# Key loads issued by ScalarE, scaled queries written in tile order by GpSimd, the factor of u by VectorE's reciprocal

## The chip, the cores and the metric

The kernel runs on one core of one Trainium2 chip. The time is that of one execution on the device, in microseconds (us). Three runs of the kernel before took 1848.44, 1849.12 and 1851.25 us, so the median is 1849.12 us. The profiled execution, from which all rows below come, took 1851.55 us. The program's instructions span 1849.8 us of it.

## What is computed

Attention over pooled keys, followed by a feed-forward layer with a SoLU activation and a layer norm. All inputs and outputs are float32 or wider (`moe_w_in` and `moe_w_out` arrive as float64).

```
kv_pool = kv.reshape(B, H//4, 4, W//4, 4, C).mean(axis=(2, 4))      # 4 batches, 768 keys of 128
k = v   = kv_pool.reshape(B, -1, C) @ w_sr
s = (q @ k.T) / sqrt(128);  a = softmax(s)                          # 12288 queries per batch
x = a @ v
h = x @ w_in;  solu = h * softmax(h)                                # 1024 columns
out = ((solu - mean) / sqrt(var + 1e-6) * g_ln) @ w_out
```

## The kernel before, in words

The 4 x 12288 queries are cut into 384 tiles of 128. Four tiles make a group (96 groups), and 96 tiles make a batch. The products are made from float16 pairs: a number is kept as a high half and a low half, and three products replace one. The first batch's scores use float32r pairs instead of float16 pairs (`wide(g)`).

One loop runs over 384 slots. In slot n several tiles are in work at different stages:

- the scores of tile n+1 (TensorE, L580), their maximum (VectorE, L601), the exponential and the high half (ScalarE, L602, L604), the low half (VectorE, L612), and a transpose of both halves by DMA, `pT<-phl` (L615);
- the product with the values for a group (TensorE, L640), written out as `xh` by ScalarE (L647) and `xl` by VectorE (L652);
- the hidden layer of tile n-9 (TensorE, L693), its maximum (VectorE, L701), its exponential `e` (ScalarE, L717), `u` = h times e times a factor per row (VectorE, L731), the halves of u (GpSimd, L748 and L755), and their transpose by DMA, `uT<-uhl` (L770);
- the last product of tile n-13 (TensorE, L821), which reads uT, and once per group the scaling and the store (L844, L853).

The order of every engine's instructions is the order in which the code records them (`manual_schedule`); nothing is rearranged, and each engine takes its instructions in that order. A DMA is also issued in the order of the engine that issues it. Before the change every DMA but one small load at the start is issued by SyncE (SP), so all share one queue: per slot one `pT` and one `uT` transpose, per group one load of queries (L528) and one store of results (L853).

While one batch is in work, the keys of the next are prepared. `kv_plan` places 16 loads of 384 KB each over the slots (`kv_load`, L225). GpSimd adds each load to a running sum in two halves (`kv_add`, L240). Six loads of the second batch (`SOON`) are issued before the loop; the other 42 stand in the loop, at the end of a slot whose number is a multiple of four, from slot 8 to slot 252. The last batch (tiles 288 to 383) has no next one, so no such loads or sums.

Three small steps belong to the change. `q_scale` (L540) multiplies a group's queries by a factor in place, contiguously, on GpSimd; `q_split` (L548, ScalarE) rounds them to float16 and `q_low` (L561, GpSimd) makes the low half. Both of the latter read the queries in steps of 128 elements (`by_tile`), so that one row of each tile stands beside those of the other three. In the first batch `q_scale` does nothing. `values_norm` (L661, GpSimd) makes two products of the softmax's sum per group, `values_recip` (L672, VectorE) inverts them, and `values_recip_u` (L678, ScalarE) multiplies one of the two by a factor `bb[:, 0:1]` to get the factor of u.

Of the kernel before, what the change touches and what calls it, by code (L numbers as in the profile page):

```python
# [67 lines left out]
def kernel(  # L68
# [38 lines left out]
    def float64_parts(raw, name):  # L107


        pair = raw.rearrange("p (f two) -> p f two", two=2)  # L110
        lo, hi = pair[:, :, 0], pair[:, :, 1]
        top = wrk.tile([P, DFF], F32, tag="u", name=f"top_{name}", bufs=5)
        if name == "in":
            rest = wrk.tile([P, DFF], F32, tag="u", name="rest_in", bufs=5)
        else:
            rest = bat.tile([P, 2 * NK], F32, tag="acc", name="rest_out", bufs=1)[:, :DFF]
        ex = wrk.tile([P, DFF], I32, tag="e", name=f"ex_{name}")
        sgn = wrk.tile([P, DFF], I32, tag="e", name=f"sgn_{name}")
        scalar = nc.vector.tensor_scalar
        both = nc.vector.tensor_tensor  # L120
        and_, shr = ALU.bitwise_and, ALU.logical_shift_right
        return top, rest, [
            partial(scalar, ex, hi, 20, 0x7FF, op0=shr, op1=and_),
            partial(scalar, ex, ex, -896.0, 0.0, op0=ALU.add, op1=ALU.max),
            partial(scalar, ex, ex, 255.0, 2.0**23, op0=ALU.min, op1=ALU.mult),
            partial(
                nc.vector.scalar_tensor_tensor,
                ex,
                hi,
                -0x80000000,  # L130
                ex,
                op0=and_,
                op1=ALU.bitwise_or,
            ),
            partial(scalar, sgn, hi, 0xFFFFF, 3, op0=and_, op1=ALU.logical_shift_left),
            partial(both, top.bitcast(I32), ex, sgn, op=ALU.bitwise_or),
            partial(
                nc.vector.scalar_tensor_tensor,
                rest,
                lo.bitcast(U32),  # L140
                2.0**-52,
                ex.bitcast(F32),
                op0=ALU.mult,
                op1=ALU.mult,
            ),
        ]
# [4 lines left out]
    def kv_alloc(b):  # L151
        for n, w, dt, bufs in (
# [3 lines left out]
            ("vf", NK, F32, 1),  # L156
        ):
            state[n, b] = bat.tile([P, w], dt, tag=n, name=f"{n}_{b}", bufs=bufs)
        for n, w in (("knm", 3), ("sv", 2), ("bb", 5), ("kq", 3), ("dg", P)):
            state[n, b] = (  # L160
                state[n, 0]
                if 0 < b < B
                else bat.tile([P, w], F32, tag=n, name=f"{n}_{b}", bufs=1)
            )
# [57 lines left out]
    def kv_first_t(half):  # L222
        nc.scalar.copy(half_of("kT", 0, half), state["pk0", half][:, :384])

    def kv_load(b, pos):  # L225

        t = dmt.tile([P, 2, 384], F32, tag="kvc", name=f"kv_{b}_{pos}", bufs=9)
        r, two = divmod(pos, 2)
        nc.sync.dma_start(
            t, kv[b - 1, r, :, two * NK : (two + 1) * NK].rearrange("p (h k) -> p h k", h=2)  # L230
        )
        state["kv", b, pos] = t
# [122 lines left out]
    def kv_bound0(part):  # L355
# [10 lines left out]
        else:  # L366
# [2 lines left out]
            small(bb[:, 2:3], bb[:, 1:2], 1e-9)  # L369
            small(bb[:, 3:4], knm[:, 2:3], 2.0**5, wsc)  # L370
            small(bb[:, 4:5], bb[:, 3:4], -1.0)
            small(sv[:, 1:2], sv[:, 1:2], knm[:, 2:3], 2.0**5 / (SC * SC))

    def kv_scale_v(b, part):
# [12 lines left out]
    def kv_bound(b, part):  # L387
# [20 lines left out]
        else:  # L408
            nc.vector.tensor_scalar(knm[:, 2:3], knm[:, 2:3], 2.0**5, None, op0=ALU.mult)
            nc.vector.tensor_scalar(bb[:, 3:4], knm[:, 2:3], wsc, None, op0=ALU.mult)  # L410
            nc.vector.tensor_scalar(bb[:, 4:5], bb[:, 3:4], -1.0, None, op0=ALU.mult)
            nc.vector.tensor_scalar(sv[:, 1:2], sv[:, 1:2], knm[:, 2:3], None, op0=ALU.mult)

    def kv_diag(b, half):
# [125 lines left out]
    def q_scale(g):  # L540
        if wide(g) or NG <= g:
            return
        qf = state["qf", g // QL][:, (g % QL) * 512 : (g % QL + 1) * 512]
        nc.gpsimd.tensor_scalar(
            qf, qf, state["kq", g // GPB][:, 1:2], 1.0, op0=ALU.mult, op1=ALU.mult
        )

    def q_split(g):  # L548
        if NG <= g < NG + GPB:
# [5 lines left out]
        else:  # L555
            qh = grp.tile([P, 512], F16, tag="qh", name=f"qh_{g}")
            ql = grp.tile([P, 512], F16, tag="ql", name=f"ql_{g}")
        nc.scalar.copy(in_tiles(qh), by_tile(qf))
        state["q", g] = (qh, ql)

    def q_low(g):  # L561
# [2 lines left out]
        qf = state["qf", g // QL][:, (g % QL) * 512 : (g % QL + 1) * 512]  # L564
        qh, ql = state["q", g]
        high = qh.bitcast(F32) if wide(g) else qh
        nc.gpsimd.tensor_tensor(in_tiles(ql), by_tile(qf), in_tiles(high), op=ALU.subtract)  # L567


    def scores_pe(t):  # L570
# [89 lines left out]

    def values_norm(g):  # L661
        b = g * GT // TPB
        zz = grp.tile([P, 2, GT], F32, tag="zz", name=f"zz_{g}", bufs=2)
        rz = grp.tile([P, 3, GT], F32, tag="rz", name=f"rz_{g}", bufs=3)
        z, bb = state.pop(("z", g)), state["bb", b]
        for k in range(2):
            nc.gpsimd.tensor_scalar(
                zz[:, k, :], z, 1e-9, bb[:, 3 + k : 4 + k], op0=ALU.add, op1=ALU.mult
            )
# [2 lines left out]
    def values_recip(g):  # L672

        zz, rz = state.pop(("zz", g))
        nc.vector.reciprocal(rz[:, 0:2, :], zz)  # L675
        state["rz", g] = [rz[:, k, :] for k in range(3)]

    def values_recip_u(g):  # L678
        rz = state["rz", g]
        nc.scalar.activation(rz[2], rz[0], AF.Copy, scale=state["bb", g * GT // TPB][:, 0:1])  # L680
        state["z2", g] = grp.tile([P, GT], F32, tag="z2", name=f"z2_{g}", bufs=3)
        state["v3", g] = grp.tile([P, GT], F32, tag="v3", name=f"v3_{g}", bufs=3)

# [208 lines left out]
        kv_first_load(*divmod(n, 8))  # L892
    q_load(1)
    for pos in SOON:
        kv_load(1, pos)
    nc.scalar.mul(w_sr16, wsr, 1.0 / RR)

    warm = ps_o.tile([P, 512], F32, tag="o", name="warm")
# [422 lines left out]
```

## Time and profile before

| what | us |
|---|---|
| median of three runs | 1849.12 |
| the profiled execution | 1851.55 |
| its span | 1849.8 |
| TensorE matmuls busy (PE) | 1821.7 |
| ScalarE busy (ACT) | 1783.7 |
| VectorE busy (DVE) | 1769.8 |
| GpSimd busy (POOL) | 1683.1 |

Busy time is a sum over the whole span. Four engines are busy for more than nine tenths of it, so the shares alone do not say which one is waited for. For that the trace is read by stretches and by waits. The source lines of the rows are those of the kernel before.

### The profile page before, as it was taken

Reading aid. Unit: us, or ns where it says so; the run is one execution under the profiler, and the core shown is the slowest. Engines: PE = TensorE matmul, PEld = TensorE weight load, DVE = VectorE, ACT = ScalarE, POOL = GpSimd, SP = SyncE. Lnnn points to the kernel's source line nnn. Section 1 sums busy time; section 2 is a strip of 40 time slices with the busy share of each in tenths; the row PEclk is TensorE's granted clock in tenths of the full one; section 3 lists DMA queues with packets and bytes.
Section 4 is the critical chain, followed back from the end, with each engine's and each line's share of the span. In section 5 each row is a group of like instructions: output and inputs, shape, how many; then the busy total and the mean of one; then the engine's idle time right before and its main releaser. Section 6 shows DMA issues by size and latency. Waiting matters only on the chain.

```text
span 1849.8 us, 42799 instructions
## 1 busy us (share of the span) xinstructions
PE 1821.7 (98%) x15747; PEld 1190.7 (64%) x15747; DVE 1769.8 (96%) x2635; ACT 1783.7 (96%) x3129; POOL 1683.1 (91%) x1466
## 2 busy tenths in 40 slices
PE   8999999999999999999999999999999999999998
PEld 5567777776566666666666666666666666666666
DVE  6999999999999999999999999999999999999997
ACT  5999999999999999999999999999999999999997
POOL 5899999899999999989999999998998989898987
PEclk9999999999999999999999999999999999999999
DMA  8999999999999999999999999999999999999998
GB/s 301 213 219 244 232 244 239 234 235 224 231 243 240 239 239 237 242 236 240 237 245 233 228 244 239 245 243 222 220 228 235 241 230 223 234 229 229 226 224 170
DMA packets 1440027, 432.80 MB, mean 234 GB/s; under 512 B 1404608, under 2 KB 1408832, under 8 KB 1439552
## 3 DMA queue, kind: packets, MB, share of 16 engines
q1 hardware_dynamic: 1439664, 429.97, 114.9%
q8 instruction: 126, 2.06, 0.5%
q14 instruction: 93, 0.76, 0.1%
q10 hardware_dynamic: 144, 0.00, 0.0%
HBM read 52.50 MB, written 25.17 MB: 42 GB/s over the span
## 4 chain that ended last, share of the span: by engine, by line
PE 66%; POOL 14%; ACT 9%; DMA 4%; issue 4%; DVE 2%; POOLq 0%; DVEq 0%
PE o L821 19%; PE h L693 18%; PE s L580 14%; PE xa L640 13%; POOL uhl L755 6%; DMA uT<-uhl 4%; POOL uhl L748 4%; ACT junk L796 2%; ACT e L717 2%; ACT s L602 2%; ACT phl L604 2%; POOL ql L567 1%; POOL ka L240 1%; PE pk L201 1%; POOL f L839 1%
## 5 line engine op out<-in xcount | busy, mean ns | idle before, releaser
L755 POOL TENSOR_TENSOR uhl<-u,uhl 128x1024 f16<-128x1024 f32 x382 | 814.5, 2133 | 31.7
L821 PEld LDWEIGHTS <-uT 128*128 128x128 f16 x9072 | 535.9, 98 | 105.3 <-DMA uT<-uhl 22.7
L821 PE MATMUL o<-wch,uT 128*128 128x128 f16 x6048 | 568.3, 219 | 10.1 <-DMA uT<-uhl 9.6
L821 PE MATMUL o<-wcl,uT 128*128 128x128 f16 x3024 | 525.9, 219 | 0.0
L731 DVE SCALAR_TENSOR_TENSOR u<-h,rz,e 128x1024 f32<-128x1024 f32 x384 | 491.1, 1279 | 26.8 <-ACT e L717 19.4
L701 DVE TENSOR_SCALAR_CACHE_REDUCE junkd<-h,rz 128x1024 bf16<-128x1024 f32 x384 | 490.8, 1278 | 1.6 <-PE h L693 1.3
L640 PE MATMUL xa<-pT,vhl 128*128 128x512 f16 x1728 | 469.5, 380 | 0.0
L748 POOL TENSOR_SCALAR uhl<-u 128x1024 f16<-128x1024 f32 x379 | 395.7, 1044 | 73.8 <-DVE u L731 65.6
L717 ACT ACTIVATE e<-h,nm,rz 128x1024 f32<-128x1024 f32 x384 | 458.6, 1194 | 3.0 <-DVE junkd L701 3.0
L796 ACT ACTIVATE junk<-u,su 128x1024 bf16<-128x1024 f32 x384 | 437.5, 1139 | 0.1
L601 DVE TENSOR_REDUCE nm<-s 128x1 f32<-128x768 f32 x384 | 364.2, 948 | 24.4 <-PE s L580 20.5
L612 DVE SCALAR_TENSOR_TENSOR phl<-s,phl 128x768 f16<-128x768 f32 x384 | 365.8, 953 | 2.9 <-ACT phl L604 2.8
L602 ACT ACTIVATE s<-s,nm 128x768 f32<-128x768 f32 x384 | 334.9, 872 | 9.7 <-DVE nm L601 9.0
L604 ACT ACTIVATE phl<-s 128x768 f16<-128x768 f32 x384 | 311.1, 810 | 12.1
L693 PEld LDWEIGHTS <-xh 128*128 128x128 f16 x1536 | 141.7, 98 | 195.0 <-DVE phl L612 33.1
L640 PEld LDWEIGHTS <-vhl 128*128 128x128 f16 x1728 | 162.7, 98 | 139.9 <-issue 12.8
L693 PE MATMUL h<-w_in_h,xh 128*128 128x512 f16 x768 | 228.9, 380 | 2.4 <-DVE rz L675 1.3
L693 PE MATMUL h<-w_in_h,xl 128*128 128x512 f16 x768 | 228.4, 379 | 0.0
L693 PE MATMUL h<-w_in_l,xh 128*128 128x512 f16 x768 | 228.4, 379 | 0.0
L580 PEld LDWEIGHTS <-qh 128*128 128x128 f16 x1152 | 107.7, 98 | 55.3 <-issue 0.7
L580 PE MATMUL s<-kh,qh 128*128 128x384 f16 x576 | 140.5, 325 | 0.6 <-DVE u L731 0.6
L580 PE MATMUL s<-kh,ql 128*128 128x384 f16 x576 | 140.7, 326 | 0.2 <-POOL ql L567 0.2
(153 smaller groups left out, 1862.7 us busy)
## 6 DMA issues: line engine op xcount, KB each, us to landing
kv<-in_kv_dram SPq DMA_DIRECT2D x64, 384.0 KB, 4.6
qf<-in_q_dram SPq DMA_DIRECT2D x96, 256.0 KB, 3.3
out_dram<-ob SPq DMA_DIRECT2D x96, 256.0 KB, 2.7
pT<-phl SPq DMA_TRANSPOSE x384, 4.0
uT<-uhl SPq DMA_TRANSPOSE x378, 4.5
raw_in<-in_moe_w_in_dram SPq DMA_DIRECT2D x1, 1024.0 KB, 5.2
raw_out<-in_moe_w_out_dram SPq DMA_DIRECT2D x1, 1024.0 KB, 9.5
room<-uhl SPq DMA_TRANSPOSE x5, 5.2
```

Source lines behind the costliest of these rows:

```text
L580: nc.tensor.matmul(s[:, half, :384], lh[:, ts], rh[:, half * 384 : (half + 1) * 384], start=n == 0, stop=n == 2,)
L602: nc.scalar.activation(s, s, AF.Exp, bias=nm, accum_out=state["z", g][:, j : j + 1])
L612: nc.vector.scalar_tensor_tensor(phl[:, 1], state.pop(("s", t)), SC, phl[:, 0], op0=ALU.mult, op1=ALU.subtract)
L640: nc.tensor.matmul(xa, v[:, c, :], pT[:, :, a * NKC + c, :], start=n == 0, stop=n == len(seq) - 1)
L693: nc.tensor.matmul(h[:, hs], lh[:, ts], rh[:, hs], start=n == 0, stop=n == 2)
L701: nc.vector.tensor_scalar(junk, state["h", t], state["rz", g][1][:, j : j + 1], None, op0=ALU.mult, op1=ALU.min, accum_out=nm,)
L717: nc.scalar.activation(e, state["h", t], AF.Exp, bias=nm, scale=state["rz", g][0][:, js], accum_out=state["z2", g][:, js],)
L731: nc.vector.scalar_tensor_tensor(u, state.pop(("h", t)), state["rz", g][2][:, j : j + 1], state.pop(("e", t)), op0=ALU.mult, op1=ALU.mult, ...
L748: nc.gpsimd.tensor_scalar(uhl[:, 0, :], u, 1.0, 1.0, op0=ALU.mult, op1=ALU.mult)
L755: low.tensor_tensor(uhl[:, 1, :], u, uhl[:, 0, :], op=ALU.subtract)
L796: nc.scalar.activation(junk, u, AF.Square, scale=-float(DFF), bias=su, accum_out=state["v3", g][:, j : j + 1],)
L821: nc.tensor.matmul(po[:, ts], uT[:, a * NFC + c, :], w[:, c, :], start=start, stop=stop)
```

## The change

Four edits, in the code:

- `kv_load` takes the issuing engine as an argument, ScalarE by default. The 42 loads in the loop are now issued by ScalarE, on its own queue; the six before the loop stay with SP.
- `q_scale` writes to a tile of its own, `qs`, in tile order; it does the strided read, and `q_split` and `q_low` read `qs` contiguously. In the first batch both still read the queries as before.
- `values_norm` makes three products instead of two, `values_recip` inverts all three, and the multiplication on ScalarE (L680) is gone. The third factor, `bb[:, 5:6]`, is made once at the start.
- The scratch tile `rest_out` at the start takes a buffer of another pool; the tile `acc`, which it used, is gone.

```
-    def kv_load(b, pos):
+    def kv_load(b, pos, eng=nc.scalar):
...
-        nc.sync.dma_start(
+        eng.dma_start(
             t, kv[b - 1, r, :, two * NK : (two + 1) * NK].rearrange("p (h k) -> p h k", h=2)
...
     for pos in SOON:
-        kv_load(1, pos)
+        kv_load(1, pos, nc.sync)
...
+        qs = grp.tile([P, 512], F32, tag="qs", name=f"qs_{g}", bufs=1)
         nc.gpsimd.tensor_scalar(
-            qf, qf, state["kq", g // GPB][:, 1:2], 1.0, op0=ALU.mult, op1=ALU.mult
-        )
+            in_tiles(qs), by_tile(qf), state["kq", g // GPB][:, 1:2], 1.0, op0=ALU.mult, op1=ALU.mult
+        )
+        state["qs", g] = qs
...
-        nc.scalar.copy(in_tiles(qh), by_tile(qf))
+        src = by_tile(qf) if wide(g) else in_tiles(state["qs", g])
+        nc.scalar.copy(in_tiles(qh), src)
...
-        nc.gpsimd.tensor_tensor(in_tiles(ql), by_tile(qf), in_tiles(high), op=ALU.subtract)
+        src = by_tile(qf) if wide(g) else in_tiles(state.pop(("qs", g)))
+        nc.gpsimd.tensor_tensor(in_tiles(ql), src, in_tiles(high), op=ALU.subtract)
...
-        zz = grp.tile([P, 2, GT], F32, tag="zz", name=f"zz_{g}", bufs=2)
+        zz = grp.tile([P, 3, GT], F32, tag="zz", name=f"zz_{g}", bufs=2)
...
-        for k in range(2):
+        for k in range(3):
...
-        nc.vector.reciprocal(rz[:, 0:2, :], zz)
+        nc.vector.reciprocal(rz, zz)
...
-        rz = state["rz", g]
-        nc.scalar.activation(rz[2], rz[0], AF.Copy, scale=state["bb", g * GT // TPB][:, 0:1])
...
+            nc.vector.reciprocal(bb[:, 5:6], bb[:, 0:1])
+            small(bb[:, 5:6], bb[:, 5:6], bb[:, 3:4])
```

On ScalarE, around slot 96, the rows before were these (`s`, `phl` and `e` are the steps of a slot, `xh` comes once per group, `rz` is the factor of u):

```order
L602 ACTIVATE s_96_6680,z_all_80<-s_96_6680,nm_96_6743 128x2x384
L604 ACTIVATE phl_96_6746<-s_96_6680 128x768
L796 ACTIVATE junk_85_6763,v3_21_6563<-u_85_6748,su_85_6749 128x1024
L717 ACTIVATE e_86_6768,z2_21_6562<-h_86_6707,nm2_86_6765,rz_21_6539 128x1024
L647 ACTIVATE xh_22_6809<-xa_22_6552,sv_0_115 128x512
L602 ACTIVATE s_97_6752,z_all_80<-s_97_6752,nm_97_6814 128x2x384
L604 ACTIVATE phl_97_6817<-s_97_6752 128x768
L796 ACTIVATE junk_86_6837,v3_21_6563<-u_86_6819,su_86_6820 128x1024
L717 ACTIVATE e_87_6842,z2_21_6562<-h_87_6776,nm2_87_6839,rz_21_6539 128x1024
L680 ACTIVATE rz_22_6831<-rz_22_6831,bb_0_116 128x4
L558 CAST qh_25_6893<-qf_25_6451 128x512
```

At the same place they are now these:

```order
L610 ACTIVATE s_96_6683,z_all_80<-s_96_6683,nm_96_6746 128x2x384
L612 ACTIVATE phl_96_6749<-s_96_6683 128x768
L802 ACTIVATE junk_85_6767,v3_21_6566<-u_85_6751,su_85_6752 128x1024
L723 ACTIVATE e_86_6772,z2_21_6565<-h_86_6710,nm2_86_6769,rz_21_6542 128x1024
L655 ACTIVATE xh_22_6813<-xa_22_6556,sv_0_115 128x512
L229 DMA kv_2_5_6816<-in_kv_dram 128x768
L610 ACTIVATE s_97_6755,z_all_80<-s_97_6755,nm_97_6818 128x2x384
L612 ACTIVATE phl_97_6821<-s_97_6755 128x768
L802 ACTIVATE junk_86_6842,v3_21_6566<-u_86_6823,su_86_6824 128x1024
L723 ACTIVATE e_87_6847,z2_21_6565<-h_87_6780,nm2_87_6844,rz_21_6542 128x1024
L565 CAST qh_25_6897<-qs_25_6765 128x512
```

The load stands directly behind `xh` and ahead of the next slot's exponential. The row of `rz` ahead of the cast is gone, and the cast reads `qs`.

On GpSimd, in the second batch, the rows before were these (`uhl` are the halves of u, `ka` is a sum of keys, `zz` are the products of `values_norm`):

```order
L748 TENSOR_SCALAR uhl_113_8801<-u_113_8790 128x1024
L755 TENSOR_TENSOR uhl_113_8801<-u_113_8790,uhl_113_8801 128x1024
L544 TENSOR_SCALAR qf_32_8491<-qf_32_8491,kq_0_117 128x512
L667 TENSOR_SCALAR zz_29_8872<-z_all_80,bb_0_116 128x4 x2
L748 TENSOR_SCALAR uhl_114_8876<-u_114_8861 128x1024
L755 TENSOR_TENSOR uhl_114_8876<-u_114_8861,uhl_114_8876 128x1024
L240 TENSOR_TENSOR ka_2_5275<-ka_2_5275,kv_2_9_8563 128x384
L748 TENSOR_SCALAR uhl_115_8954<-u_115_8944 128x1024
L755 TENSOR_TENSOR uhl_115_8954<-u_115_8944,uhl_115_8954 128x1024
L567 TENSOR_TENSOR ql_32_8937<-qf_32_8491,qh_32_8936 128x512
```

Now they are these:

```order
L754 TENSOR_SCALAR uhl_113_8811<-u_113_8800 128x1024
L761 TENSOR_TENSOR uhl_113_8811<-u_113_8800,uhl_113_8811 128x1024
L549 TENSOR_SCALAR qs_32_8814<-qf_32_8500,kq_0_117 128x512
L675 TENSOR_SCALAR zz_29_8883<-z_all_80,bb_0_116 128x4 x3
L754 TENSOR_SCALAR uhl_114_8888<-u_114_8872 128x1024
L761 TENSOR_TENSOR uhl_114_8888<-u_114_8872,uhl_114_8888 128x1024
L240 TENSOR_TENSOR ka_2_5277<-ka_2_5277,kv_2_9_8573 128x384
L754 TENSOR_SCALAR uhl_115_8965<-u_115_8955 128x1024
L761 TENSOR_TENSOR uhl_115_8965<-u_115_8955,uhl_115_8965 128x1024
L575 TENSOR_TENSOR ql_32_8948<-qs_32_8814,qh_32_8947 128x512
```

No row moved; the products are three instead of two, and `qs` stands between the queries and their halves.

On SP the rows before, around a load, were these:

```order
L528 DMA qf_21_5272<-in_q_dram 128x512
L615 DMA_TRANSPOSE pT_19_5306<-phl_76_5280 128x12x128
L770 DMA_TRANSPOSE uT_65_5340<-uhl_65_5293 128x16x128
L229 DMA kv_2_2_5345<-in_kv_dram 128x768
L615 DMA_TRANSPOSE pT_19_5306<-phl_77_5350 128x12x128
L770 DMA_TRANSPOSE uT_66_5420<-uhl_66_5367 128x16x128
```

Now they are these:

```order
L532 DMA qf_21_5274<-in_q_dram 128x512
L623 DMA_TRANSPOSE pT_19_5308<-phl_76_5282 128x12x128
L776 DMA_TRANSPOSE uT_65_5342<-uhl_65_5295 128x16x128
L623 DMA_TRANSPOSE pT_19_5308<-phl_77_5352 128x12x128
L776 DMA_TRANSPOSE uT_66_5422<-uhl_66_5370 128x16x128
```

Only the load is gone from between the transposes.

## Rows read from the trace of the kernel before

**Rows 1.** Three stretches by the exponential of L717: start:end, length, busy (instructions), clock, DMA share, GB/s

```profile
56.20:512.00 455.80, 123.34 (x192) 1.00 1.17 232
512.00:1413.50 901.50, 246.79 (x384) 1.00 1.19 237
1413.50:1634.10 220.60, 61.73 (x96) 1.00 1.14 232
```

**Rows 2.** Waits from 512 to 1413.5: who waits for whom, us, times, longest

```profile
POOL uhl L748 <- DVE u L731: 25.9, 31, 2.2
...
PEld L821 <- DMA uT<-uhl: 16.2, 21, 1.9
...
DVE u L731 <- ACT e L717: 10.2, 42, 0.5
...
PE o L821 <- DMA uT<-uhl: 6.8, 14, 1.4
```

**Rows 3.** Waits from 56.2 to 512

```profile
POOL uhl L748 <- DVE u L731: 12.2, 15, 2.3
```

**Rows 4.** Waits from 1413.5 to 1634.1

```profile
POOL uhl L748 <- DVE u L731: 14.1, 11, 1.3
```

**Rows 5.** SP's DMA issues around one load: start, length, what

```profile
1047.64 1.42 SPq L615 DMA_TRANSPOSE pT<-phl  x1
...
1056.11 0.57 SPq L229 DMA_DIRECT2D kv<-in_kv_dram  x1
...
1058.32 4.53 SPq L770 DMA_TRANSPOSE uT<-uhl  x1
```

**Rows 6.** GpSimd there, in order of time

```profile
1050.83 0.61 POOL L667 TENSOR_SCALAR zz<-z_all,bb 128x4 f32<-128x4 f32 x2
1051.52 1.04 POOL L748 TENSOR_SCALAR uhl<-u 128x1024 f16<-128x1024 f32 x1
1052.65 2.13 POOL L755 TENSOR_TENSOR uhl<-u,uhl 128x1024 f16<-128x1024 f32 x1
```

**Rows 7.** TensorE there, with the wait ahead of it

```profile
1065.14 0.23 PE L821 MATMUL o<-wch,uT 128*128 128x128 f16 x1 [1.37 <-DMA uT<-uhl]
```

**Rows 8.** DMA from 1050 to 1070 in 40 slices of 0.5 us: busy tenths, GB/s

```profile
DMA  9999948999999994189999990099999999299999
GB/s 276 275 288 288 271 106 302 270 242 290 273 166 290 255 180 43 25 295 359 236 196 289 303 51 4 10 256 291 344 356 275 140 296 92 39 283 282 291 282 291
```

**Rows 9.** Groups of instructions by line, GpSimd: busy, mean ns of one | idle before

```profile
L567 POOL TENSOR_TENSOR ql<-qf,qh 128x512 f16<-128x512 f32 x72 | 101.3, 1407 | 0.0
...
L544 POOL TENSOR_SCALAR qf<-qf,kq 128x512 f32<-128x512 f32 x72 | 49.5, 688 | 0.0
...
L274 POOL TENSOR_TENSOR kl<-kT,kh 128x384 f16<-128x384 f32 x6 | 5.5, 916 | 0.0
```

**Rows 10.** Groups by line, ScalarE

```profile
L558 ACT CAST qh<-qf 128x512 f16<-128x512 f32 x72 | 80.0, 1112 | 0.0
...
L680 ACT ACTIVATE rz<-rz,bb 128x4 f32<-128x4 f32 x96 | 27.6, 287 | 0.8 <-DVE rz L675 0.8
...
L746 ACT CAST uhl<-u 128x1024 f16<-128x1024 f32 x4 | 4.2, 1038 | 0.0
L271 ACT CAST kh<-kT 128x384 f16<-128x384 f32 x6 | 3.0, 500 | 0.0
```

**Rows 11.** Groups by line, VectorE

```profile
L675 DVE RECIPROCAL rz<-zz 128x8 f32<-128x8 f32 x96 | 18.5, 193 | 1.4 <-POOL zz L667 1.2
```

**Rows 12.** The start, SP

```profile
0.73 0.39 SPq L880 DMA_DIRECT2D wsr<-in_w_sr_dram  x1
```

**Rows 13.** The start, ScalarE

```profile
0.73 0.40 ACTq L882 DMA_DIRECT2D gl<-in_moe_g_ln_dram  x1
```

**Rows 14.** ScalarE at the place where the load of rows 5 will stand

```profile
1047.97 0.68 ACT L647 ACTIVATE xh<-xa,sv 128x512 f16<-128x512 f32 x1
1048.54 0.87 ACT L602 ACTIVATE s<-s,nm 128x768 f32<-128x768 f32 x1
```

More of the change, by code (lines that the diff above doesn't have):

```diff
@@ L115, in float64_parts @@
         else:
-            rest = bat.tile([P, 2 * NK], F32, tag="acc", name="rest_out", bufs=1)[:, :DFF]
+            rest = dmt.tile([P, DFF], F32, tag="uhl", name="rest_out", bufs=5)
         ex = wrk.tile([P, DFF], I32, tag="e", name=f"ex_{name}")
@@ L158, in kv_alloc @@
             state[n, b] = bat.tile([P, w], dt, tag=n, name=f"{n}_{b}", bufs=bufs)
-        for n, w in (("knm", 3), ("sv", 2), ("bb", 5), ("kq", 3), ("dg", P)):
+        for n, w in (("knm", 3), ("sv", 2), ("bb", 6), ("kq", 3), ("dg", P)):
             state[n, b] = (
@@ L411, in kv_bound @@
             nc.vector.tensor_scalar(bb[:, 4:5], bb[:, 3:4], -1.0, None, op0=ALU.mult)
+            nc.vector.reciprocal(bb[:, 5:6], bb[:, 0:1])
+            nc.vector.tensor_scalar(bb[:, 5:6], bb[:, 5:6], bb[:, 3:4], None, op0=ALU.mult)
             nc.vector.tensor_scalar(sv[:, 1:2], sv[:, 1:2], knm[:, 2:3], None, op0=ALU.mult)
```

## The prediction

> **What bounds the kernel now.** The page's busy times name no bound: four engines are near full. So I read stretches first, then waits, then one place in order of time.
>
> The stretches [rows 1] give the time of a slot. L717 runs one exponential per tile, and each leaves two instructions (the second reads its sum), so 192, 384 and 96 instructions are 96, 192 and 48 slots. That is 455.8 / 96 = 4.748 us per slot while the first batch's tiles pass the hidden layer, 901.5 / 192 = 4.695 us for the second and third, and 220.6 / 48 = 4.596 us in the fourth. The second and third cost 192 x (4.695 - 4.596) = 19.1 us more than at the pace of the fourth. In that stretch the fourth has neither loads of keys nor sums of them, and both sides have the same queries, scores and hidden layers. The list of waits of the fourth has four lines, of which [rows 4] show the first; none of them is for uT. In the second and third TensorE waits for `uT` in 14 matmuls for 6.8 us and its weight loads wait 21 times for 16.2 us [rows 2].
>
> One place shows how such a wait arises. GpSimd ends the halves of one tile at 1052.65 + 2.13 = 1054.78 [rows 6]. SP issues their transpose only at 1058.32, 3.5 us later, because a load of keys goes first in SP's order (1056.11), and its issue lasts 4.53 us [rows 5]. TensorE gets the tile at 1065.14, 1.37 us late [rows 7]. The rates of the DMA engines in that time [rows 8] hold the cause: slices 15 and 16, from 1057.5 to 1058.5, move 43 and 25 GB/s where 270 to 300 is usual, directly ahead of the two slices of 295 and 359 in which the load's data come. [...] That is about 1 us lost per load, beside the 0.39 MB itself, which at those two rates takes about 1.2 us. So the late transposes behind loads are what I expect to go.
>
> GpSimd stands in the way. In the 901.5 us it waits for u only 25.9 us [rows 2], so it is occupied for (901.5 - 25.9) / 192 = 4.560 us of each slot. In the fourth batch it waits 14.1 us in 220.6 [rows 4]. GpSimd is 0.04 us per slot under the pace of 4.596 us, and the change gives it work.
>
> **The change, part by part.**
>
> Loads. 42 issues leave SP and go to ScalarE. What stood behind the load in SP's queue goes ahead: its two transposes start 0.6 us earlier (the issue took 0.57 [rows 5]), and the pause of about 1 us in the data is open to transposes. TensorE's wait for uT is at least 6.8 us. The rows of a matmul end later than the engine is free for the next one (0.23 us long in rows 7, while the ends are modelled), so up to the 16.2 us of the weight loads may count [rows 2]. I take 10, near the lower row plus about 0.15 us for each of 21 waits. Gross: -10.
>
> On ScalarE the issue stands behind `xh` and ahead of the next exponential. `xh` begins at 1047.97, the exponential at 1048.54 [rows 14], so 0.57 us of execution can cover an issue of 0.57 us. If ScalarE can't issue under a running instruction, 42 x 0.57 = 24 us of ScalarE are the price. What waits behind it is the exponential, `phl`, then `e`, on which VectorE's u waits. The load has one wait of its own, for the DMA eight places earlier in the program; that is the uT transpose of three tiles before, so I put it at 0; were it late, ScalarE would stand still with the same queue behind it. At the start of the program SP and ScalarE issue a load each at the same 0.73, and they take 0.39 and 0.40 us [rows 12, 13]: neither waits for the other. The Trainium skill, "Perfetto Trace Analysis", section "DMA Instruction — HWDGE (DVE, Sync)", says that the unit that makes the descriptors is locked for one issuer at a time, and that the wait for the lock lies in the profiled length; the trace's two rows at 0.73 do not show such a wait, but they are no transposes. In the middle of the loop SP is issuing a transpose at the moment of ScalarE's turn: 1047.64 + 1.42 - 1047.97 = 1.09 us would be left of it [rows 5, 14], or 42 x 1.09 = 46 us in all. I take 0, by the nearer rows 12 and 13, and keep the 46 as a rival.
>
> GpSimd. A third product per group: two take from 1050.83 to 1051.52 [rows 6], so one more is 0.34 us, 96 x 0.34 = 33 us in all, of which 48 x 0.34 = 16.3 fall into the second and third batch, 8.2 into the first. `q_low` reads contiguously: its row is 1407 ns for 512 columns; the like instruction for 384 columns takes 916 [rows 9], so 512 take at most 916 x 4/3 = 1221, and with 2133 for 1024 [rows 6] on the line through both, 1159. That is 0.25 us less. `q_scale` now reads in steps, and no row has this. It costs at least nothing (688 ns stay [rows 9]); at most I put ScalarE's surcharge for the same read: its cast is 1112 in steps against 500 for 384 and 1038 for 1024 columns without, which gives 608 for 512 [rows 10], so 0.50 us. I take GpSimd's own surcharge, 0.25, so these two edits cancel. Together 48 x 0.34 = 16.3 against 25.9 of waits: 16.3 / 192 = 0.085 per slot, 4.560 + 0.085 = 4.645. If GpSimd never waited, the stretch would take 4.645 x 192 = 891.8 us, 9.7 less than now. That is the most that the loads can give there. Its waits don't lie where its work is, so I let half of the gross gain come back: -5 in this stretch, between -9.7 and 0.
>
> In the first batch GpSimd has 12.2 us of waits [rows 3] for 8.2 us of new work, and `q_scale` isn't run. TensorE is slower there by itself (float32r scores). I put +1, between -3 and +4. In the fourth, 12 groups x 0.34 = 4.1 us stand against waits of 14.1 [rows 4]: 0.
>
> ScalarE and VectorE. ScalarE loses 96 x 0.287 = 27.6 us (L680) and 72 x 0.50 = 36 us of casts [rows 10]. VectorE waits for ScalarE's `e` for 10.2 us [rows 2]; what of this ends a slot later is small, as 42 waits average 0.24 us. I put -2, between -5 and 0. VectorE's reciprocal has 12 columns instead of 8: between nothing and half of 193 ns more [rows 11], at most 96 x 0.10 = 9 us, and I take 0, as 10.2 us of VectorE's waits cover it.
>
> Start. One more reciprocal and one more product, in turn on VectorE and GpSimd, once: +0.5. The scratch tile moves no instruction: 0.
>
> Sum: -5 + 1 + 0 - 2 + 0.5 = -5.5. Against the profiled execution that is 1851.55 - 5.5 = 1846.0. It stood 2.4 us over the median of the runs, so the forecast for the median is 1843.6.
>
> **The rivals.**
>
> *No gain from the queue.* The Trainium skill, "DMA: Bandwidth & Descriptors", section "Issuing engines are not separate DMA queues", says that DMAs from different engines run on the same 16 DMA engines and interleave, and that a second issuer saves only the sequencer's time. By that rule the transposes lose the load's time wherever it is issued; rows 8 speak for it in the data's two slices, and against it in the pause ahead of them. As a mechanism here: the load runs into the transposes of its own slot, some 8 us earlier than now (1047.97 against 1056.11), and uT comes late at another place. Then the -5 is gone, and the time is 1849.1 + 1 - 2 + 0.5, about 1848.6.
>
> *GpSimd becomes the bound.* At `q_scale` the stepped read costs the 0.50 of ScalarE's row, so 0.25 net per group and 0.34 for the product make 0.59 us x 48 = 28 us, over the 25.9 of waits [rows 2]. From 25.9 / 48 = 0.54 us per group on it decides even if no wait is left. With half of the waits staying, as they follow stalls elsewhere, the stretch takes 28 - 13 = +15 us, the first batch 8.2 - 6.1 = +2, and -2 for ScalarE: 1849.1 + 15, about 1864. For it: the 4.560 us of occupied time per slot. Against: a faster path behind GpSimd (3.5 us in rows 5, 6) lets it be late for some slots without TensorE's noticing.
>
> *ScalarE is held by SP's transposes.* Each issue waits the 1.09 us of above. A group saves 0.29 + 0.50 = 0.79 on ScalarE, so 0.3 us per load remain on average, 13 us in 42 loads, and they pass to `e`, u and TensorE: 1849.1 - 5 + 13 + 1, about 1858. It decides from about 0.8 us per issue on.
>
> **How the numbers follow.** The forecast gets 0.47, no gain from the queue 0.23, GpSimd as the bound 0.18, ScalarE held 0.10, anything else 0.02. The forecast's own range is from 1849.1 - 9.7 - 3 - 5, about 1832, to 1849. The upper end takes in the held ScalarE and most of the bound GpSimd: 1832 to 1861. A difference under 0.2% (3.7 us) is what a measurement of this kernel can't tell from none: the limits are 1845.4 and 1852.8. The forecast is below 1845.4 in four of five cases and the no-gain rival in one of three, which makes 0.45 faster; the last two rivals and a little of the second make 0.29 slower; 0.26 stay the same.
>
> **What would show it.** In the profile after: the waits of TensorE and its weight loads for uT in the second and third batch fall under 3 and 6 us; SP issues the transpose of u within about 1 us of GpSimd's end; the slices ahead of a load's data have no pause. The issue on ScalarE lasts about 0.6 us, and no wait is put down to it. `q_scale` takes about 0.94 us, `ql` 1.16, the cast of `qh` 0.61. GpSimd's waits for u in that stretch fall from 25.9 to about 10 to 15. A slot there takes about 4.67 us, and in the fourth batch 4.596 as before. I would be wrong if uT's waits stay (first rival), if GpSimd's waits fall to nothing with slots of 4.7 us or more (second), or if issues on ScalarE last over 1 us (third).

## The result: slower by 0.9%, because GpSimd became the bound

The changed kernel took 1865.22 us (median of four runs, 1864.36 to 1867.1), the kernel before 1848.78 us beside it (1847.02 to 1851.25). The ratio is 1.0089, with a 95% interval from 1.0072 to 1.0107. The forecast was 1843.6 us in a range that ended at 1861. The time is that of my second rival, GpSimd as the bound, which I had priced at about 1864 and given 0.18; the range ended 3 us under this price. Of the 23 executions of the kernel before that the ratios of e5 to e8 below go by, one took 7816.68 us and is left out; no trace of it was kept.

The stretches come first, by the same exponential (now L723), with the columns of [rows 1] except that PE's clock stands behind ACT's busy time.

```profile
56.30:513.80 457.50, 123.33 (x192) 1.00 1.15 233
513.80:1425.90 912.10, 246.74 (x385) 1.00 1.16 234
1425.90:1647.10 221.20, 61.67 (x96) 1.00 1.15 230
```

The first grew by 1.7 us, the second by 10.6, the third by 0.6. The profiled span grew from 1849.8 to 1862.9, by 13.1, and these three hold 12.9 of it. (The medians differ by 16.4; the profiled execution before was 2.4 us over its median.) So the loss lies where GpSimd has all of its work, in the second and third batch: 912.1 / 192 = 4.751 us per slot.

The waits from 513.8 to 1425.9 answer to [rows 2].

```profile
ACT s L610 <- DVE nm L609: 50.8, 49, 2.7
...
DVE rz L683 <- POOL zz L675: 15.3, 16, 2.0
...
DVE u L737 <- ACT e L723: 9.2, 49, 0.5
PE s L588 <- DVE u L737: 8.8, 16, 0.6
PEld L588 <- POOL ql L575: 8.2, 23, 0.4
...
POOL uhl L754 <- DVE u L737: 6.7, 8, 1.3
```

No line for uT is left, as was wanted; but e7 below has none worth naming either, with the loads back on SP, so their move is not what ended these waits. GpSimd's waits for u fell from 25.9 to 6.7 us, so it is occupied for (912.1 - 6.7) / 192 = 4.716 us of each slot, over the 4.596 of the fourth batch. This figure counts GpSimd's short gaps as occupied. Its busy time in the same stretch, the last of the five engines below, rose by 26.1 us, from 843.30 to 869.44 (PE, PEld, DVE, ACT, POOL, each with its instructions; before and then after):

```profile
512.00:1413.50 901.50, 892.08 (x7821) 567.21 (x7819) 873.61 (x1297) 885.32 (x1560) 843.30 (x734) 1.00 1.19 237
```

```profile
513.80:1425.90 912.10, 898.37 (x7814) 566.80 (x7813) 878.12 (x1297) 855.07 (x1514) 869.44 (x783) 1.00 1.16 234
```

Others now wait for GpSimd: VectorE's reciprocal for the products, the weight loads of the scores for `ql`. ScalarE's wait for VectorE rose from 3.7 to 50.8 us: its own work fell by 30.3 us, and the stretch is 10.6 us longer.

The chain that ended last tells the same, before and then after (shares of the span by engine).

```profile
PE 66%; POOL 14%; ACT 9%; DMA 4%; issue 4%; DVE 2%; POOLq 0%; DVEq 0%
```

```profile
POOL 41%; PE 24%; DVE 12%; issue 11%; ACT 11%; DMA 2%; POOLq 0%; DVEq 0%; ACTq 0%
```

GpSimd's groups by line after (columns as in [rows 9]):

```profile
L549 POOL TENSOR_SCALAR qs<-qf,kq 128x512 f32<-128x512 f32 x72 | 86.4, 1200 | 0.0
...
L575 POOL TENSOR_TENSOR ql<-qs,qh 128x512 f16<-128x512 f32 x72 | 83.6, 1160 | 0.0
L675 POOL TENSOR_SCALAR zz<-z_all,bb 128x4 f32<-128x4 f32 x288 | 77.0, 267 | 24.3
```

`ql` fell from 1407 to 1160 ns, as forecast. The scaling rose from 688 to 1200, where I had taken 0.94 us. The products stand with 24.3 us of idle time ahead of them for which the trace names nobody: 84 ns ahead of each of the 288. Before it was 88 ns ahead of each of 192 (16.9 us), so each further product brings its gap along.

One place shows both sides, near that of [rows 5 to 7]. First GpSimd in order of time (start, length), then SP's issues, then ScalarE's.

```profile
1058.42 2.13 POOL L761 TENSOR_TENSOR uhl<-u,uhl 128x1024 f16<-128x1024 f32 x1
1060.55 1.20 POOL L549 TENSOR_SCALAR qs<-qf,kq 128x512 f32<-128x512 f32 x1
1061.84 0.95 POOL L675 TENSOR_SCALAR zz<-z_all,bb 128x4 f32<-128x4 f32 x3
1062.88 1.04 POOL L754 TENSOR_SCALAR uhl<-u 128x1024 f16<-128x1024 f32 x1
1064.01 2.13 POOL L761 TENSOR_TENSOR uhl<-u,uhl 128x1024 f16<-128x1024 f32 x1
1066.10 0.99 POOL L240 TENSOR_TENSOR ka<-ka,kv 128x384 f32<-128x384 f32 x1
1067.08 1.04 POOL L754 TENSOR_SCALAR uhl<-u 128x1024 f16<-128x1024 f32 x1
```

```profile
1055.46 3.33 SPq L776 DMA_TRANSPOSE uT<-uhl  x1
...
1060.90 3.00 SPq L776 DMA_TRANSPOSE uT<-uhl  x1
...
1066.17 1.58 SPq L776 DMA_TRANSPOSE uT<-uhl  x1
```

```profile
1058.40 0.33 ACTq L229 DMA_DIRECT2D kv<-in_kv_dram  x1
```

GpSimd has no gap over 0.1 us. Two halves of u begin 1064.01 - 1058.42 = 5.59 us apart, because `qs` and the three products lie between. SP issues the transposes 0.35 and 0.03 us after GpSimd's ends at 1060.55 and 1066.14, where it was 3.5 us at the place of [rows 5 and 6]. There the load was the smaller part: SP was busy with the transpose of the tile before until 1056.05, and then with the load (0.57 us) and the scores' transpose:

```profile
1053.59 2.46 SPq L770 DMA_TRANSPOSE uT<-uhl  x1
...
1056.79 1.43 SPq L615 DMA_TRANSPOSE pT<-phl  x1
```

Over the second and third batch the median from GpSimd's last end to SP's issue of uT is 2.5 us before, 1.3 with the loads moved alone (e1), 0.35 in the changed kernel and 0.36 in e7, where the loads are on SP. So SP waits for GpSimd now chiefly because GpSimd is later. ScalarE's load begins while SP is issuing (1055.46 + 3.33 = 1058.79) and still takes 0.33 us; the 42 take 334 to 354 ns each. So my third rival, ScalarE held by SP's transposes, is out.

### The profile page after: what moved, and what is told of

It reads as the page before. It is cut to its first block, busy times and chain, and to the rows that moved or that the text cites. A ratio compares the mean times of both kernels' runs of the same rounds, so it can differ in the third digit from the quotient of the medians.

```text
span 1862.9 us, 42800 instructions
## 1 busy us (share of the span) xinstructions
PE 1831.2 (98%) x15747; PEld 1191.0 (64%) x15747; DVE 1776.3 (95%) x2636; ACT 1735.2 (93%) x3033; POOL 1726.8 (93%) x1563
## 4 chain that ended last, share of the span: by engine, by line
POOL 41%; PE 24%; DVE 12%; issue 11%; ACT 11%; DMA 2%; POOLq 0%; DVEq 0%; ACTq 0%
POOL uhl L761 17%; POOL uhl L754 10%; PE o L827 6%; PE h L699 6%; PE s L588 5%; PE xa L648 5%; ACT e L723 3%; POOL ka L240 3%; ACT junk L802 3%; DVE junkd L707 3%; DVE nm L609 3%; POOL f L845 3%; ACT phl L612 3%; POOL qs L549 2%; DVE phl L620 2%
## 5 line engine op out<-in xcount | busy, mean ns | idle before, releaser
L723 ACT ACTIVATE e<-h,nm,rz 128x1024 f32<-128x1024 f32 x384 | 458.5, 1194 | 3.3 <-DVE junkd L707 3.3
```

Of the source, the lines that this page charges most:

```text
L723: nc.scalar.activation(e, state["h", t], AF.Exp, bias=nm, scale=state["rz", g][0][:, js], accum_out=state["z2", g][:, js],)
```

## Experiments

Theory G says that GpSimd sets the pace of the changed kernel, and that the loads on ScalarE are harmless. Its rivals: S, the loads on ScalarE cost the time; A, each edit has a price of its own and the prices add; Q, the scaled queries come late for ScalarE and the scores. The table has all runs by one working, for the second and third batch of the profiled execution: length of the stretch, GpSimd's waits for u in it, and (length - waits) / 192 as GpSimd's occupied time per slot. Ratios are against the runs of the kernel before that each run had beside it. Every stretch is that of one execution, while executions of one kernel lie up to 20 us apart: those shown of e8, e9 and e10 took 1840.53, 1842.61 and 1843.53 us, 3 to 8 us under their medians, that of the kernel before 1851.55. Differences of a few us between single stretches are therefore not shown by them.

| run | median us | ratio, 95% | stretch | waits for u | occupied |
|---|---|---|---|---|---|
| before | 1848.78 | | 901.5 | 25.9 | 4.560 |
| changed | 1865.22 | 1.0089 [1.0072, 1.0107] | 912.1 | 6.7 | 4.716 |
| e1 loads alone | 1846.61 | 0.9984 [0.9967, 1.0] | 899.4 | 22.4 | 4.568 |
| e2 product alone | 1857.1 | 1.0037 [1.0024, 1.005] | 904.5 | 10.4 | 4.657 |
| e3 order alone | 1851.5 | 1.0004 [0.9995, 1.0014] | 902.6 | 12.9 | 4.634 |
| e4 steps in the write | 1867.01 | 1.0093 [1.0078, 1.0108] | 913.3 | 6.4 | 4.723 |
| e5 loads, product | 1855.89 | 1.0043 [1.0027, 1.0059] | 901.8 | 9.2 | 4.649 |
| e6 loads, order | 1847.55 | 0.9994 [0.9981, 1.0007] | 899.2 | 9.9 | 4.632 |
| e7 product, order | 1866.51 | 1.009 [1.0077, 1.0104] | 912.9 | 6.6 | 4.720 |
| e8 changed, one product | 1848.17 | 0.9982 [0.9962, 1.0002] | 894.8 | 37.4 | 4.466 |
| e9 loads, one product | 1846.28 | 0.9983 [0.9964, 1.0001] | 896.3 | 50.0 | 4.408 |
| e10 as e8, loads on SP | 1846.48 | 0.9985 [0.9971, 0.9998] | 896.6 | 39.7 | 4.463 |
| e11 before, few loads | (two passes) | | 891.5 | 15.0 | 4.565 |
| e12 as e8, few loads | (two passes) | | 889.2 | 33.0 | 4.459 |

**e1_loads_only.** The kernel before with one edit:

```
-        nc.sync.dma_start(
+        eng.dma_start(          # eng=nc.scalar; the six loads ahead of the loop stay with SP
```

> The kernel before with one edit: the 42 loads in the loop are issued by ScalarE. Theory G (GpSimd sets the pace of the changed kernel, the loads are harmless): GpSimd stays occupied 4.56 us per slot, under TensorE's 4.596, and the waits of TensorE for uT go, so 1838 us, between 1833 and 1846, with 4.62 us per slot in the second and third batch. Rival S (the loads on ScalarE are what costs): slower than before, about 1865. Rival N (same 16 DMA engines, no gain): 1847 to 1851.

It took 1846.61 us, between a small gain and none, and between the two ranges: 0.6 over G's, 0.4 under N's. GpSimd's 4.568 is as G said, but the waits for uT did not go. The move shows no cost, against S. The stretch is 2.1 us shorter, not the 10 that I had as the gross gain. In four more pairs that differ by the loads' place alone (e2 and e5, e3 and e6, e7 and the changed kernel, e10 and e8) it is 2.7, 3.4, 0.8 and 1.8 us shorter: always the same way, always small. The first half of the second batch runs at the fourth batch's pace, 220.6 / 48 = 4.596 us per slot; the stalls come behind it.

```profile
510.00:730.60 220.60, 61.68 (x96) 1.00 1.20 243
730.60:1409.40 678.80, 185.14 (x288) 1.00 1.19 234
```

Waits in both together:

```profile
PEld L821 <- DMA uT<-uhl: 8.5, 7, 3.3
PE o L821 <- DMA uT<-uhl: 5.7, 3, 2.8
```

Against [rows 2] the waits are fewer (7 and 3 times for 21 and 14) and longer (up to 3.3 us for 1.9). The transposes still come late, only elsewhere.

**e2_product_only.** The kernel before with three products and no multiplication on ScalarE:

```
-        for k in range(2):
+        for k in range(3):
...
-        nc.scalar.activation(rz[2], rz[0], AF.Copy, scale=state["bb", g * GT // TPB][:, 0:1])
```

> The kernel before with one edit: GpSimd makes the third product and VectorE's reciprocal gives the factor of u; ScalarE's multiplication is gone. Theory G: GpSimd is occupied 4.56 + 0.085 = 4.645 us per slot and the waits for uT behind loads stay, so 1849 + 5 to 10, about 1856. Rival S: ScalarE is relieved, so 1845 to 1849.

1857.1 us, as G said: this edit alone has a price. GpSimd's occupied time rose by 0.097 us per slot, 0.39 us per group; I had read 0.34 from [rows 6].

**e3_order_only.** The kernel before with `qs` in tile order:

```
-            qf, qf, state["kq", g // GPB][:, 1:2], 1.0, op0=ALU.mult, op1=ALU.mult
+            in_tiles(qs), by_tile(qf), state["kq", g // GPB][:, 1:2], 1.0, op0=ALU.mult, op1=ALU.mult
```

> The kernel before with one edit: GpSimd writes the scaled queries in tile order into a tile of its own (and the scratch tile at the start sits elsewhere). Theory G: q_scale takes 1.20 instead of 0.69 us, q_low 1.16 instead of 1.41, so GpSimd is occupied 0.26 / 4 = 0.066 us longer per slot, 4.626; with the waits behind loads 1849 + 3 to 8, about 1854. Rival S: ScalarE's cast falls by 0.50 us per group, so 1843 to 1849.

1851.5 us, between the ranges of S and G, and no change that can be told from none, although the stepped read costs what it costs in the whole change (GpSimd's group):

```profile
L545 POOL TENSOR_SCALAR qs<-qf,kq 128x512 f32<-128x512 f32 x72 | 86.6, 1203 | 0.0
```

The 0.30 us per group more (4.634 against 4.560) went into GpSimd's waits, 25.9 to 12.9.

The step of this read needs a correction: `by_tile` takes every fourth element, those of one tile, so the step is 4 elements or 16 bytes, and not the 128 elements that I wrote ahead of the prediction and in the expectation of e4.

**e4_write_steps.** The changed kernel; the scaling reads contiguously and writes in steps of four elements. As written this puts the queries into another order than `q_split` takes them to be in, so it computes something else; the instructions and their sizes are the same.

```
-            in_tiles(qs), by_tile(qf), ...
+            qs.rearrange("p (j t) -> p t j", t=GT), qf.rearrange("p (t j) -> p t j", t=GT), ...
```

> The changed kernel with one edit: q_scale reads the queries contiguously and writes qs in steps of four elements, instead of reading in steps of 128 and writing contiguously. Theory G: if writing in steps costs GpSimd nothing (0.69 us), it is occupied 4.56 + 0.085 - 0.062 = 4.583 us per slot, TensorE sets the pace again, 1838 to 1845; if it costs what the read in steps costs (1.20 us), 1865 as the changed kernel. Rival S: 1865 either way.

```profile
L549 POOL TENSOR_SCALAR qs<-qf,kq 128x512 f32<-128x512 f32 x72 | 87.8, 1219 | 0.0
```

1219 ns and 1867.01 us. A step of 16 bytes on the writing side costs as much as one on the reading side. Whether another order of the loop saves the edit stays open: the contiguous read that keeps the right order writes in steps of 128 elements, and no run has that.

**e5_no_order, e6_no_product, e7_no_loads.** The changed kernel with one edit undone in each: the scaling as before, the products as before, and the loads back on SP.

```
e5: +            qf, qf, state["kq", g // GPB][:, 1:2], 1.0, op0=ALU.mult, op1=ALU.mult
e6: +        for k in range(2):     # and ScalarE's multiplication by bb[:, 0:1]
e7: +        nc.sync.dma_start(
```

> The changed kernel with the scaled queries written in place and contiguously again; the loads on ScalarE and the third product on GpSimd stay. Theory G (GpSimd sets the pace: its work is 4.560 us per tile before, TensorE's own pace is 4.596): 4.560 + 0.34/4 = 4.645 per tile in the second and third batch, 1850 to 1855 us, GpSimd's waits for u below the 36 us that the product alone left. Rival A (each edit has a price of its own and the prices add: -3.7, +6.8 and +1.2 us as measured alone): 1850.3 - 3.7 + 6.8 = 1853.4 us. The two don't differ much here; their sum over the three pairs does. Rival S (the loads on ScalarE cost time as soon as another edit is beside them): 1860 us or more.

> The changed kernel with ScalarE's multiplication by the bound as before and two products on GpSimd; the loads on ScalarE and the order of the scaled queries stay. Theory G: 4.560 + (0.512 - 0.247)/4 = 4.626 us per tile, just above TensorE's 4.596: 1847 to 1852 us. Rival A: 1850.3 - 3.7 + 1.2 = 1847.8 us. Rival S: 1860 us or more.

> The changed kernel with the loads issued by SP again; both edits on GpSimd stay. Theory G: GpSimd's 4.560 + (0.34 + 0.512 - 0.247)/4 = 4.71 us per tile is over what TensorE and SP allowed before (4.695), so the loads don't matter: 1862 to 1868 us, with slots of 4.71 to 4.75 us in the second and third batch, as in the changed kernel. Rival A: 1850.3 + 6.8 + 1.2 = 1858.3 us. Rival S: 1858 us or less, since the loads on ScalarE are gone.

They took 1855.89, 1847.55 and 1866.51 us. The sums of single prices (A) are 1853.4, 1847.8 and 1858.3: good for the first two, 8.2 us short for the third. e7 is as slow as the whole change, with the loads where they were, so S falls, and the same stretch is found, with next to nothing left of the waits for uT (matmuls have none):

```profile
514.30:1427.20 912.90, 246.80 (x385) 1.00 1.15 233
```

```profile
PEld L827 <- DMA uT<-uhl: 0.4, 1, 0.4
```

The prices don't add because the slack is one: alone, product and order took 15.5 and 13.0 of the 25.9 us that GpSimd waited (to 10.4 and 12.9 left), and together they would take more than there is. It stops at 6.6. G's times for e6 and e7 held; e5 came 0.9 us over its range.

A rival not named ahead of these runs is that the products come late for VectorE's reciprocal, which waits 15.3 us for them in the changed kernel. Against it: this wait is 7.4 us in e5 and 7.7 in e6, while e6 costs nothing and e5 6 us. What differs the right way is GpSimd's occupied time, 4.649 and 4.632.

**e8_one_product.** The changed kernel with one instruction for the three products (the 1e-9 is left out of the sum, which is at least 1):

```
-        for k in range(3):
-            nc.gpsimd.tensor_scalar(
-                zz[:, k, :], z, 1e-9, bb[:, 3 + k : 4 + k], op0=ALU.add, op1=ALU.mult
-            )
+        nc.gpsimd.tensor_tensor(
+            zz,
+            z.unsqueeze(1).to_broadcast([P, 3, GT]),
+            bb[:, 3:6].unsqueeze(2).to_broadcast([P, 3, GT]),
+            op=ALU.mult,
+        )
```

> The changed kernel with one instruction on GpSimd (128x12, both operands broadcast) in place of the three products of 128x4 (3 x 267 ns); everything else stays, the strided scaling too. Estimate for the one: about 0.3 us, so GpSimd does 0.5 us less per group: 4.735 - 0.125 = 4.61 us per tile. Theory G: slots fall from 4.735 to 4.60 to 4.65 us and the time to 1848 to 1853 us, although nothing of the strided scaling and of the loads is undone. Rival Q (the long scaling is late for ScalarE's cast and for the scores, so the path through the queries sets the pace): 1862 us or more.

GpSimd's groups by line:

```profile
L549 POOL TENSOR_SCALAR qs<-qf,kq 128x512 f32<-128x512 f32 x72 | 86.8, 1205 | 0.0
...
L674 POOL TENSOR_TENSOR zz<-z_all,bb 128x12 f32<-128x12 f32 x96 | 20.4, 213 | 0.0
```

1848.17 us: 17 us of the change's price are gone, with the stepped scaling (1205 ns) and the loads as they are. Q falls, and the time goes with GpSimd's load alone, as G said (G's range for the slot ended at 4.65; it took 894.8 / 192 = 4.660). VectorE's wait for the products goes too, from 15.3 to 0.3 us; e5 and e6 speak against it as the cause. The instruction took 213 ns, and the idle time ahead of it is 0.0 where the three had 24.3 us: 3 x 267 + 24300 / 96 - 213 = 841 ns per group, of the (4.716 - 4.466) x 4 = 1.0 us that GpSimd was relieved by. Its waits for u are back, and so are those for uT.

```profile
POOL uhl L756 <- DVE u L739: 37.4, 40, 2.3
...
PEld L829 <- DMA uT<-uhl: 8.7, 8, 2.6
PE o L829 <- DMA uT<-uhl: 4.9, 6, 2.1
```

**e9_loads_one_product.** e1 with the one instruction of e8, the queries scaled as before:

> The kernel before with the loads on ScalarE and one instruction on GpSimd (128x12, measured 213 ns) in place of its two products and of ScalarE's multiplication by the bound; the scaled queries stay in place and contiguous. Theory G: GpSimd does 4.560 + (0.213 - 2 x 0.306)/4 = 4.46 us per tile, well under TensorE's 4.596, so the time is that of the loads alone or a little less: 1840 to 1847 us; what is left over 4.596 are stalls for uT at the end of the stretches with loads. Rival T (with GpSimd free, TensorE and the transposes' queue set the pace alone, and GpSimd's further 0.13 us per tile against the run with one product and the strided scaling buy nothing): the same 1848 us within 2.

1846.28 us, which both expectations allowed. GpSimd waits 50.0 us instead of 37.4, and neither the median nor the stretch (896.3 us against 894.8) can be told from e8's. No gain from more relief for GpSimd is shown, as T said.

**e10_one_product_sp.** e8 with the loads on SP:

> The changed kernel with one product of 128x12 and with the loads issued by SP: only the place of the loads differs from the run that came to 1848.2 us. If the loads on ScalarE are worth something once GpSimd isn't the bound (my prediction's first term), the slots in the stretches with loads go back to about 4.69 us and the time is 2 to 6 us above that run: 1850 to 1854 us, with TensorE's waits for uT back at 14 us or more in the second and third batch. If they are worth nothing (the transposes are held by the DMA engines, not by their place behind the loads): 1846 to 1849 us and the same waits for uT (8.7 us).

```profile
PEld L829 <- DMA uT<-uhl: 15.1, 20, 1.5
...
PE o L829 <- DMA uT<-uhl: 6.8, 10, 1.0
```

1846.48 us, with e8's ratio inside its interval. The waits for uT came back as the first expectation said (21.9 us against e8's 13.6), the time did not rise as it said. The stretch is 896.6 - 894.8 = 1.8 us longer, and the median is 1.7 us shorter, so no price of the loads' place is shown here. SP's issue of uT comes 2.5 us after GpSimd's end in the median, against 1.3 in e8: with GpSimd relieved, the move does shorten the wait in SP's order, and TensorE gains almost nothing by it. This is the one variant whose interval lies wholly under 1 against the kernel before (0.9971 to 0.9998). It isn't told apart from e8 and e9, whose runs spread over 17 us; it is faster than the changed kernel.

**e11_before_few_loads, e12_one_product_few_loads.** The kernel before, and e8, with 39 of the 42 loads left out:

```
+        if pos and (b, pos) not in [(1, p) for p in SOON]:
+            state["kv", b, pos] = state["kv", b, 0]
+            return
```

> The kernel before with 39 of the 42 loads of the next batches' keys left out (each later addition takes the batch's first tile again): part of the computation is left out, every other instruction stays. What the loads cost at all, by their issue on SP and by their bytes in the DMA engines. The prediction priced them at 4.695 - 4.596 = 0.099 us per tile in the stretches with loads, 5 us per batch in the second and third: 1839 to 1843 us and no waits of TensorE for uT to speak of. Rival: the stretches are long for another reason, and the time stays within 3 us of 1849.

> The changed kernel with one product of 128x12 and with 39 of the 42 loads of the next batches' keys left out (as in the other run of this job; part of the computation is left out). Theory D (with GpSimd free, the loads' bytes in the DMA engines hold the transposes, from whichever queue they are issued): slots of 4.60 us in the whole of the second and third batch and 1834 to 1839 us, 8 us or more below the 1848 and 1846 us with the loads on ScalarE and on SP. Rival: the loads' bytes are hidden, and it stays at 1844 to 1849 us with slots of 4.65 us.

Neither total can be used: 7387.24 and 7379.08 us. With such keys the condition at the end of the program (`n < P`, L1290 of the changed kernel) sends it into `general()`, which computes all tiles again (768 exponentials instead of 384). The first pass is a run of the loop like the others, and its stretch can be compared, for e11 and then e12.

```profile
509.80:1401.30 891.50, 246.87 (x385) 1.00 1.15 228
```

```profile
507.90:1397.10 889.20, 246.87 (x384) 1.00 1.16 228
```

No wait for uT is listed in either. The loads cost 901.5 - 891.5 = 10.0 us in the kernel before. With GpSimd relieved they cost 894.8 - 889.2 = 5.6 us from ScalarE and 896.6 - 889.2 = 7.4 from SP. These are differences of single executions and rough by several us; what they do show is that the waits for uT go with the loads, and not with the loads' place in SP's order. That the rest of the price is their share of the DMA engines, as D has it, is argued and not shown.

D also wanted 4.60 us for every slot, while 889.2 / 192 is 4.631. The record shows why: TensorE has next to no idle time there. It is busy for 888.35 of the 889.20 us in e12, as it is for all of the fourth batch before (columns as in the five-engine rows above):

```profile
507.90:1397.10 889.20, 888.35 (x7813) 567.57 (x7812) 871.73 (x1297) 852.86 (x1513) 836.38 (x686) 1.00 1.16 228
```

```profile
1413.50:1634.10 220.60, 220.60 (x1946) 140.68 (x1944) 217.48 (x325) 219.08 (x385) 198.02 (x175) 1.00 1.14 232
```

The second and third batch have 36 matmuls that the fourth has not, the products that make the next batch's keys and values (e12's lines):

```profile
L443 PE MATMUL s<-ka,w_sr 128*128 128x128 f32 x24 | 3.6, 274 | 0.0
L452 PE MATMUL s<-dg,kT 128*128 128x128 f32 x12 | 1.8, 274 | 0.0
```

They are 5.4 of the 889.2 - 192 x 4.596 = 6.8 us. So TensorE's own pace in the second and third batch is 888.35 / 192 = 4.627 us per slot, not the 4.596 that the prediction and the theories above go by. This also fits the table: with GpSimd occupied for 4.632 and 4.634 us (e6, e3) no loss is seen, from 4.649 on (e5, e2, the changed kernel) there is one.

## Why the prediction was wrong

*The step that failed* is "I take GpSimd's own surcharge, 0.25, so these two edits cancel". The surcharge was that of `ql`, which reads two operands; the scaling reads one. It measured 1200 - 688 = 512 ns against 247 saved, that is the upper bound that I had written down (0.50, from ScalarE). That the number of operands makes the difference is a guess from these two instructions. The Trainium skill, "GPSIMD Engine Reference", section "Performance pitfalls for Q7 kernels", says that a read whose step is over 8 bytes costs half as much again; the step here is 16 bytes, the rows show 74%, and e4 shows 77% for a stepped write, of which that section says nothing. By the page's half, an estimate, the scaling would have taken 688 x 1.5 = 1032 ns, more than I took: with the product that makes 0.44 us per group, still under the 0.54 at which GpSimd decides.

With the scaling and the product GpSimd got (4.716 - 4.560) x 4 = 0.62 us per group, and the rival had said from where on it decides: 0.54. 48 x 0.62 = 30 us don't fit into 25.9. The product was 0.39 us of it, where I had 0.34.

*A second term failed beside it*, the -5 for the stretch. e5 is the change with the two order edits at nothing, as I had summed them, and it took 1855.89 us: 12.3 of the 21.6 us between forecast and result are there without the scaling, which makes the other 9.3. I had let half of a gross gain of 9.7 us come back, so GpSimd would have kept 4.8 us of its waits; in e5 it kept 9.2, and the stretch was 0.3 us longer than before instead of 5 shorter. The move of the loads gave back about 2 us in the stretch and not 10. The 19.1 us over the fourth batch's pace were no measure for it: 5.4 of them are the matmuls that e12 shows, which no queue gives back. That "its waits don't lie where its work is" was right: e2 lost 6.8 us with 10.4 us of waits left. In the changed kernel 6.7 were left, where the rival had 13; so its +15 for the stretch became +10.6.

*Loads.* Cost of the issue at 0: right (334 ns, no wait put down to it, SP issuing at the same time). The Trainium skill, "Perfetto Trace Analysis", section "DMA Instruction — HWDGE (DVE, Sync)", has an issuer wait for a lock; the row of 0.33 us at 1058.40, inside SP's issue, shows no such wait. The late transposes went, but by luck: e7, as slow on GpSimd, has none with the loads on SP, and in e1, where only the loads moved, 14.2 of 23.0 us of waits stayed. The gross 10 us are about what the loads cost altogether (e11), not what their queue costs: the move alone gave 2.1 in the stretch, and 1.8 with GpSimd relieved. The pause that I read from [rows 8] as 1 us lost per load isn't the loads' either: slices 23 to 25 of the same rows (51, 4, 10 GB/s) have no load ahead of them, and of the slices of 0.5 us in the second and third batch 170 of 1800 are under 60 GB/s before and 211 of 1760 in e11. My first rival was right on this term. The Trainium skill, "DMA: Bandwidth & Descriptors", section "Issuing engines are not separate DMA queues", has it so. The medians of e8 and e10 (1848.17 and 1846.48) agree; only the waits for uT differ, 13.6 and 21.9 us.

*ScalarE, -2*: no run shows it. What ScalarE saved it spent waiting for VectorE (50.8 us in the stretch). *First batch, +1*: it was 1.7. *Fourth, 0*: 0.6. *Start, +0.5*: the first exponential came 0.1 us later.

*What would show it*: TensorE's waits, SP's issue within 1 us at the place shown, no pause ahead of the data of the load issued at 1058.40 (214 to 292 GB/s from 1058 to 1060), `ql` and the cast (607 ns) came as said, the first two not for the reason given. The issue on ScalarE took 0.33 us, not 0.6; the fourth batch 221.2 / 48 = 4.608 us per slot. `q_scale` at 0.94, GpSimd's waits at 10 to 15 and a slot of 4.67 did not come, and the last two didn't fit each other: 4.67 x 192 - 891.8 leaves 4.8 us of waits. The text had named "GpSimd's waits fall to nothing with slots of 4.7 us or more" as the sign of the rival.

What stays open: what the 84 ns ahead of each short product are, why a stepped access costs the scaling so much more than `ql`, how the loads delay the transposes, and why executions of e8 and e9 lie up to 17 us apart.

## What to carry to other kernels

Where an engine has a little less occupied time per step than the bound, add up everything that a change gives it and compare the sum with its waits in that stretch; edits that cost 7 and 1 us alone (e2, e3) cost 17 together (e7). Where no row has the surcharge of an access pattern for an instruction with as many operands, let its upper end decide whether the engine crosses the bound. Take the pace of the bound from the same stretch: the fourth batch's 4.596 left out matmuls that the second and third have. What a transfer costs is found by leaving it out, not by moving it: moving it to another queue gave back 2 us of some 10 here. And a wait that goes after a change has not gone by it until a run without that edit still has the wait (e7).

## What the runs showed of the hardware that wasn't expected

- On GpSimd one 128x512 float32 product by a column took 688 ns contiguously, 1200 read in steps of 16 bytes and 1219 written in steps of 16 bytes (e4).
- One GpSimd instruction of 128x12 with both operands broadcast took 213 ns (e8), with no idle time ahead of it; a 128x4 product by a column took 267, with 84 ns of idle time ahead of each in the changed kernel, so that three cost GpSimd about 1.05 us.
- The issue of the same load took 334 to 354 ns on ScalarE in the loop, 327 to 341 ns on SP ahead of the loop, and 0.57 us on SP in the loop, at the place of [rows 5].
- The kernels with GpSimd as the bound repeat within 3 us in four or five runs each (changed, e4, e7), five of the others within 10 to 20 us in eleven or twelve (e1, e6, e8, e9, e10) and e3 within 6 in twelve. Whether the bound makes the spread is not shown.
- Pauses in the DMA engines' data, slices of 0.5 us under 60 GB/s, were no rarer with 39 of 42 loads left out than with them: 211 of 1760 (e11) against 170 of 1800.
